# Lagged first layer with row scales from sums of squares, and a last block that finishes one token half early

## The chip, the core and the metric

The program runs on one core of a Trainium2 chip. The core's engines work from queues of their own: TensorE (PE in the profile, with its weight loads as PEld) multiplies, VectorE (DVE) and ScalarE (ACT) work on whole tiles, GpSimd (POOL) issues the indirect DMAs and some small steps, SyncE (SP) issues the other DMAs. The metric is device microseconds of one execution; lower is better. Times of stretches are microseconds from the start of the profiled span.

## The reference

Attention with landmarks over 8 batches and 8 heads gives 4608 rows of 512. A routed layer follows: each row goes to the one of 8 experts with the largest gate value. Then comes a dense layer with a squared ReLU.

```python
x = attention(q, k, v)                       # 4608 x 512
idx = argmax(x @ w_gate, axis=1); g = softmax(x @ w_gate)[idx]
for e in range(8):                           # first layer, D = 512, F = 1024
    out[idx == e] = g * (relu(x[idx == e] @ w1[e]) @ w2[e])
h = relu(out @ w_in)                         # second layer, F = 2048
y = (h * h) @ w_out
```

## The kernel before, in words

Every number of a matrix is kept as two float16 halves, high and low, so a product takes three matmuls: high by high, high by low, low by high.

The attention (`phase_a`) writes the rows to DRAM (`x_rows`) and works out a sorted order of rows by expert. It also runs two tiles of 128 rows of the first layer by itself ("the earlier tiles", names z, zvn, zkn).

`phase_m1` is the first layer: one step for each further tile of 128 rows, tile 2 to 37 with this data, 36 in all. The last two stand under run-time conditions. In a step, for tile j:

- GpSimd gathers the rows of tile j+3 (`gather`, L80).
- `prep` for tile j+2: a row scale from the largest magnitude (`rowscale`, L56 to L60, on DVE), the high half xh on ACT (L90), the low half on DVE (L92).
- SP turns the input of tile j+1 by a DMA transpose (`turn_dma`, L108). Tile 2 is turned on PE (`turn`, L101, L103).
- `mm1` (L120 to L122): 96 matmuls of 128 columns in two groups (hf 0 and 1). Behind each group ACT writes the high half of hT (L125, with the ReLU) and DVE the low half (L126).
- `mm2` (L135): 24 matmuls of 512 columns into py. For the first four hT tiles it runs high by high, low by high, high by low; for the other four, high by high, high by low, low by high.
- `post` for tile j-1: ACT takes py out with the gate (yg, L143), DVE finds a row scale from the largest magnitude (L56 to L60), ACT writes the high half (L149), DVE the factor (L153 to L156) and the low half (L157), GpSimd scatters the row tile into `x2` (L158).
- `change(j+1)`: where the next tile has another expert, ACT and DVE convert the staged weights (`conv`, L1045 and L1046, eight pieces each) into the one weight buffer wb, and SP loads the next expert's weights into the staging buffer. The condition is read at run time; with this data it holds at four tiles.
- `fill`: the second layer's weights come in as 64-bit numbers and are split beside the first layer, one load per step, in a generator in four parts (`wide_split`, L1065 to L1091): ACT clears the sign (fg), DVE builds the float32 bits, GpSimd makes sums of weight quarters (fq, L1087), ACT and DVE write the two halves.

Each engine works its queue strictly in the order in which the step emits; `go` and `run` advance the generators, so the order of those calls is the order of every queue.

`phase_m2` is the second layer: 18 blocks of 256 rows, 8 pairs of column groups per block, each with 24 matmuls (L1136 to L1138). `pair` squares the result and builds seven combinations hq; `piece`, two pairs later, multiplies them by seven weight combinations into seven sums (L1158); `result` adds the sums into two token halves and GpSimd scatters each half (`put`, L1174). The first block's input is loaded during the first layer (`first`, tile 16).

Of the kernel before, what the change touches and what calls it, by code (L numbers as in the profile page):

```python
# [52 lines left out]
def rowscale(nc, al, out, src, k, tag):  # L53
# [13 lines left out]
             pt=([128, 8, 128], F16), ph=([128, 4, 128], F32), py=([128, DM], F32))  # L67


class Layer1:  # L70
# [57 lines left out]
    def mm2(self, s):  # L128
        hT, (wh, wl) = s["hT"], self.w2
        s["py"] = py = self.al("py")  # L130

        hh, hl, lh = (0, wh), (0, wl), (1, wh)
        ps = [(f, *x) for f0, xs in ((0, (hh, lh, hl)), (4, (hh, hl, lh))) for x in xs for f in range(f0, f0 + 4)]
        for i, (f, a, w) in enumerate(ps):
            self.nc.tensor.matmul(py, hT[:, a, f], w[:, f], start=(i == 0), stop=(i == len(ps) - 1))  # L135
            if i % 4 == 3:
                yield

    def post(self, s, to, tok):
# [19 lines left out]
                                     in_=xr, in_offset=None)  # L159

# [775 lines left out]
def phase_m1(tc, cst, x_rows, x2, w1, w2, rt, stg, wb, fill, first):  # L936
    nc = tc.nc
    identh = cst["identh"]
    with (
        tc.tile_pool(name="m1", bufs=1, reuse_waits="tile") as m1,  # L940
        tc.tile_pool(name="m3", bufs=3, reuse_waits="tile") as m3,
        tc.tile_pool(name="m4", bufs=4, reuse_waits="tile") as m4,
        tc.tile_pool(name="m5", bufs=7, reuse_waits="tile") as m5,
        tc.tile_pool(name="mph", bufs=2, space=PSUM, reuse_waits="tile") as mph,
        tc.tile_pool(name="mpy", bufs=3, space=PSUM, reuse_waits="tile") as mpy,
# [17 lines left out]
        def change(j):  # L963
# [5 lines left out]
            for i in range(2):  # L969
                load(s["nx"], s["ld"], i)  # L970

        pools = dict(xg=m4, xm=m3, s1=m5, xh=m3, gt=m5, xT=m3, hT=m1, yg=m1, ym=m3, s2=m3, ss=m3, xr=m1,
                     ph=mph, py=mpy)
        L = Layer1(nc, cst, wb, x2, lambda nm: mph.tile(*TILES[nm], tag="ph", name=nm) if nm == "pt" else pools[nm].tile(*TILES[nm], tag=nm, name=nm))
# [13 lines left out]
        for j in range(PT, PT + 3):  # L988
            gather(j)
        for j in range(PT, PT + 2):  # L990
            run(L.prep(st[j]))
        run(L.turn(st[PT]))
        change(PT)
        idle = iter(())
        fls = [idle]
# [3 lines left out]

        def step(j):  # L1000
            last = j + 1 == NTL
            tail = j >= NTF
            po = L.post(st[j - 1], rt["sidx"][:, j - 1:j], rt["gidx"][:, j - 1:j]) if PT < j < NTF else idle
            pr = L.prep(st[j + 2]) if j + 2 < NTL else idle
            old, fl = fls.pop(), iter(() if tail else fill(j) or ())
            fls.append(fl)
            if not last:
                L.turn_dma(st[j + 1])
            if j == 4 + NE + PT + 2:
                first()  # L1010
            go(po, pr, po, fl)
            run(L.mm1(st[j], 0))
            if j + 3 < NTL:
                gather(j + 3)
            go(po)
            go(old, pr, po)
            run(L.mm1(st[j], 1))
            run(L.mm2(st[j]))
            if not last:
                change(j + 1)  # L1020
            go(fl, old, pr, fl)
            if j + 1 >= NTF:
                go(*(4 * [L.post(st[j], rt["sidx"][:, j:j + 1], rt["gidx"][:, j:j + 1])]))
# [32 lines left out]
def wide_split(tc, pool, w, scale, dst, quad=None):  # L1056
# [7 lines left out]
    g = pool.tile([128, 512], I32, tag="fg", name="fg")  # L1064
    nc.scalar.activation(g.bitcast(F32), hi.bitcast(F32), AF.Abs)  # L1065

    m = pool.tile([128, 512], I32, tag="fm", name="fm", bufs=1)
    V.tensor_scalar(m, lo, 29, 7, op0=ALU.logical_shift_right, op1=ALU.bitwise_and)
    yield
# [3 lines left out]
    yield  # L1073
# [29 lines left out]
def load_block(nc, pool, x2, blk):  # L1103

    n = TB // 128
    xT = pool.tile([128, 8, TB], F16, tag="x2T", name="x2T")
# [8 lines left out]
def phase_m2(tc, x2, wi, wo, first, out):  # L1115
# [4 lines left out]
    with (  # L1120
# [31 lines left out]
        def piece(b, f):  # L1152

            hq = ps[8 * b + f]["hq"]
            for k, (a, w) in enumerate(PRODS):
                for i, (u, x) in enumerate(((0, 0), (0, 1), (1, 0))):

                    PE.matmul(sums[k // 2][:, k % 2], hq[:, u, a], wo[:, x, f, w], start=(f == 0 and i == 0 and k % 2 == 0),  # L1158
                              stop=(f == 7 and i == 2), skip_group_check=True)

        def result(b):
# [4 lines left out]
            r = [n2.tile([128, TB], F32, tag=f"r{i}", name=f"r{i}") for i in range(3)]  # L1166
            p1, p6, p7, p5, p4, p3, p2 = (sums[k // 2][:, k % 2] for k in range(7))
# [4 lines left out]
            def put(t):  # L1172
                ACT.activation(o[t], o[t], AF.Copy, scale=sc[t])  # L1173
# [113 lines left out]
```

## Time and profile before

| | |
|---|---|
| time, three runs | 1443.92, 1450.49, 1451.67 us (median 1450.49) |
| profiled execution | 1445.92 us, span 1444.2 us |
| mean granted TensorE clock | 0.977 |
| busy share of the span | PE 94%, PEld 75%, DVE 72%, ACT 40%, POOL 19% |
| first layer, tile 2 to 37 | 290.5 to 716 us |
| second layer | 721 to 1433 us |

A timeline row gives the start, the duration, the engine, the line and the instruction with the tile it writes and the tiles it reads. The brackets give the idle time of that engine just before and what ended it. With several instructions merged (x8), the duration is from the first's start to the last's end. Successive instructions of an engine overlap a little, so their starts lie closer than their durations.

### The profile page before, as it was taken

How to read it: one execution, taken by the hardware profiler on the slowest of the kernel's cores; microseconds unless marked ns; L12 is line 12 of the kernel's file. 1: busy time of each engine (PE TensorE's matmuls, PEld its weight loads, DVE VectorE, ACT ScalarE, POOL GpSimd, SP SyncE). 2: the span in 40 equal slices, each digit the busy share in tenths (PEclk: the TensorE clock that was granted, in tenths of full speed). 3: DMA queues.
4: the chain of work that ended last, by engine and by line, in shares of the span. 5: the costliest groups of instructions: out<-in, count | busy, mean ns of one | idle time of the engine just before them, and what ended most of it. 6: DMA issues, size and time to landing. Idle time of an engine off the chain costs nothing. (4 is left out here: it accounts for less than half of the span.)

```text
span 1444.2 us, 35176 instructions
## 1 busy us (share of the span) xinstructions
PE 1352.3 (94%) x14312; PEld 1077.5 (75%) x14312; DVE 1040.5 (72%) x2651; ACT 575.8 (40%) x979; POOL 274.1 (19%) x282
## 2 busy tenths in 40 slices
PE   5999889889898997899899999999999999999996
PEld 4555555667575775667688888888888888888886
DVE  5888998858888887989556666666666666666664
ACT  4555565333553353443333333333333333333332
POOL 4434563111111223132200000000000000000000
PEclk9999999999999999999999999999999999999999
DMA  8767674476758547364310111111111101111100
GB/s 197 164 162 187 158 175 94 122 190 126 212 119 224 131 123 205 87 132 102 72 33 16 30 31 31 30 23 24 29 30 30 30 19 27 30 31 30 30 9 22
DMA packets 133695, 127.05 MB, mean 88 GB/s; under 512 B 90832, under 2 KB 109264, under 8 KB 133520
## 3 DMA queue, kind: packets, MB, share of 16 engines
q1 hardware_dynamic: 123680, 94.45, 28.5%
q0 software_dynamic: 9200, 30.21, 6.7%
q8 instruction: 114, 1.87, 0.6%
q14 instruction: 61, 0.50, 0.1%
q10 hardware_dynamic: 640, 0.02, 0.0%
HBM read 219.49 MB, written 28.89 MB: 172 GB/s over the span
## 5 line engine op out<-in xcount | busy, mean ns | idle before, releaser
L1158 PE MATMUL o<-wo,hq 128*128 128x256 f16 x3024 | 356.1, 272 | 0.0
L1158 PEld LDWEIGHTS <-hq 128*128 128x128 f16 x3024 | 295.6, 98 | 37.3 <-issue 2.8
L1136 PE MATMUL h<-x2T,wi 128*128 128x256 f16 x1152 | 314.8, 273 | 5.0 <-ACTq L1037 5.0
L1138 PE MATMUL h<-x2T,wi 128*128 128x256 f16 x1152 | 314.7, 273 | 0.0
L1137 PE MATMUL h<-x2T,wi 128*128 128x256 f16 x1152 | 314.7, 273 | 0.0
L1148 ACT ACTIVATE hq<-q 128x896 f16<-128x896 f32 x144 | 136.8, 950 | 289.9 <-DVE q L1146 289.9
L1150 DVE SCALAR_TENSOR_TENSOR hq<-q,hq 128x896 f16<-128x896 f32 x144 | 157.1, 1091 | 129.0 <-ACT hq L1148 129.0
L135 PE MATMUL py<-wb,hT 128*128 128x512 f16 x864 | 202.3, 392 | 22.2 <-DVE ss L153 16.3
L120 PE MATMUL ph<-xT,wb 128*128 128x128 f16 x1152 | 196.9, 220 | 8.7 <-DMA xT<-xh 6.8
L122 PE MATMUL ph<-xT,wb 128*128 128x128 f16 x1152 | 196.9, 220 | 3.4 <-DVE wb L1046 3.2
L121 PE MATMUL ph<-xT,wb 128*128 128x128 f16 x1152 | 196.9, 220 | 0.0
L1174 POOL DMA_INDIRECT out<-out,fa x36 | 54.5, 1514 | 665.3 <-ACT out L1173 590.6
L135 PEld LDWEIGHTS <-hT 128*128 128x128 f16 x864 | 84.9, 101 | 124.0 <-DVE hT L126 18.2
L1142 DVE TENSOR_TENSOR q<-q 128x512 f32<-128x512 f32 x144 | 99.5, 691 | 92.6 <-ACT q L1141 92.6
L1141 ACT ACTIVATE q<-h 128x512 f32<-128x512 f32 x144 | 85.4, 593 | 139.7 <-PE h L1138 139.7
L120 PEld LDWEIGHTS <-wb 128*128 128x128 f16 x1216 | 119.6, 98 | 14.8 <-issue 3.8
L1137 PEld LDWEIGHTS <-wi 128*128 128x128 f16 x1152 | 113.0, 98 | 16.2 <-issue 2.9
L1136 PEld LDWEIGHTS <-wi 128*128 128x128 f16 x1152 | 113.0, 98 | 15.7 <-SPq L1037 2.5
L1138 PEld LDWEIGHTS <-wi 128*128 128x128 f16 x1152 | 113.0, 98 | 13.4
L122 PEld LDWEIGHTS <-wb 128*128 128x128 f16 x1216 | 119.6, 98 | 4.4 <-DVE wb L1046 4.4
L121 PEld LDWEIGHTS <-wb 128*128 128x128 f16 x1216 | 119.6, 98 | 4.0
L126 DVE SCALAR_TENSOR_TENSOR hT<-ph,hT 128x512 f16<-128x512 f32 x72 | 49.7, 690 | 61.0 <-ACT hT L125 31.0
(289 smaller groups left out, 1904.8 us busy)
## 6 DMA issues: line engine op xcount, KB each, us to landing
stg<-in_moe_w SPq DMA_DIRECT2D x76, 2048.0 KB
qn<-in_q SPq DMA_DIRECT2D x16, 576.0 KB
kn<-in_k SPq DMA_DIRECT2D x16, 576.0 KB
vn<-in_v SPq DMA_DIRECT2D x16, 576.0 KB
fw<-in_moe_w_in SPq DMA_DIRECT2D x16, 512.0 KB
fw<-in_moe_w_out SPq DMA_DIRECT2D x16, 512.0 KB
x_rows<-xr SPq DMA_DIRECT2D x32, 192.0 KB
stg<-in_moe_w SPq DMA_DIRECT2D x16, 256.0 KB
```

Of the source, the lines that this page charges most:

```text
L120: nc.tensor.matmul(ph[:, f4], wh[:, c, fs], xT[:, c], start=(c == 0), stop=False)
L121: nc.tensor.matmul(ph[:, f4], wh[:, c, fs], xT[:, 4 + c], start=False, stop=False)
L122: nc.tensor.matmul(ph[:, f4], wl[:, c, fs], xT[:, c], start=False, stop=(c == 3))
L135: self.nc.tensor.matmul(py, hT[:, a, f], w[:, f], start=(i == 0), stop=(i == len(ps) - 1))
L1136: PE.matmul(ph[:, z], wi[:, 0, c, fs], xT[:, c], start=(c == 0), stop=False)
L1137: PE.matmul(ph[:, z], wi[:, 0, c, fs], xT[:, 4 + c], start=False, stop=False)
L1138: PE.matmul(ph[:, z], wi[:, 1, c, fs], xT[:, c], start=False, stop=(c == 3))
L1141: ACT.activation(q[:, 3:7], ph.rearrange("p z (t n) -> p (z t) n", t=2), AF.Relu, scale=2.0 ** -7)
L1142: V.tensor_tensor(q[:, 3:7], q[:, 3:7], q[:, 3:7], op=ALU.mult)
L1148: ACT.activation(hq[:, 0], q, AF.Copy, scale=0.5)
L1150: V.scalar_tensor_tensor(hq[:, 1], q, 0.5, hq[:, 0], op0=ALU.mult, op1=ALU.subtract)
L1158: PE.matmul(sums[k // 2][:, k % 2], hq[:, u, a], wo[:, x, f, w], start=(f == 0 and i == 0 and k % 2 == 0), stop=(f == 7 and i == 2), skip_ ...
```

## The change

`Stream1` replaces `Layer1` in `phase_m1`. The row scales come from sums of squares: ACT squares a row tile and adds up each row (`norm`), DVE makes two powers of two out of the sum by integer steps (`scales`), for one tile's input and another tile's output in one go. The output is no longer kept in yg: both halves are written from py with gate times scale. Gathers run four tiles ahead and scatters two behind, the turn by DMA two ahead, and PE turns tiles 2 and 3. `gate`, the factor and the token number move from DVE to GpSimd. Pools change with it: py 4, ph 3, fg 3.

```diff
-        ps = [... for f0, xs in ((0, (hh, lh, hl)), (4, (hh, hl, lh))) for x in xs for f in range(f0, f0 + 4)]
+        ps = [(f, *x) for x, f0 in ((hh, 0), (hl, 0), (hh, 4), (hl, 4), (lh, 0), (lh, 4)) for f in range(f0, f0 + 4)]
...
+    def norm(self, src, sq, i, scale=1.0):
+        self.nc.scalar.activation(self.al("jk"), src, AF.Square, scale=scale, accum_out=sq[:, i:i + 1])
+    def scales(self, sq, i, n, nm="s4"):
...
+        V.tensor_scalar(v, v, 1, 0x7F800000, op0=ALU.logical_shift_right, op1=ALU.bitwise_and)
+        V.tensor_scalar(o[:, i:i + n], v, -1.0, float(197 << 23), op0=ALU.mult, op1=ALU.add)
+        V.tensor_scalar(o[:, 2 + i:2 + i + n], v, 1.0, float(57 << 23), op0=ALU.mult, op1=ALU.add)
...
+    def yhigh(self, s):
+        s["xr"] = self.al("xr")
+        self.nc.scalar.activation(s["xr"][:, 0:DM], s["py"], AF.Copy, scale=s["gs"][:, 0:1])
+    def ylow(self, s):
+        xr = s["xr"]
+        self.nc.vector.scalar_tensor_tensor(xr[:, DM:2 * DM], s.pop("py"), s["gs"][:, 0:1], xr[:, 0:DM], ...)
...
         def step(j):
...
+            elif j + 4 < FAR:
+                gather(j + 4)
...
+            if j == NTF - 1:
                 first()
+            if PT + 2 <= j < NTF:
+                scatter(j - 2)
+            if j + 3 < FAR:
+                L.gate(st[j + 3])
+            up = [L.up(s, 0)]
+            go(up[0])
...
+                L.norm(st[j - 1]["py"], sq(j), 0, st[j - 1]["gt"][:, 0:1])
+                norm_x(j + 3)
+                L.low(st[j + 2])
+            go(fl)
...
+                s4 = L.scales(sums.pop(j), 0 if ny else 1, int(ny) + int(nx))
+                    L.out_scale(st[j - 1], nc.gpsimd)
...
+            up.append(L.up(s, 1))
+            go(up[1])
+            if j + 2 < NTF + 2:
+                L.turn_dma(st[j + 2])
+            run(L.mm2(s))
             if not last:
                 change(j + 1)
+            go(old, old)
+                L.yhigh(st[j - 1])
+                L.high(st[j + 3])
...
+            go(fl)
+                L.ylow(st[j - 1])
```

(The conditions `if ny`, `if nx` before some of these lines are left out here.) In `wide_split` the first `yield` moves ahead of DVE's first instruction, and a later one goes.

In the second layer, the last block is emitted in another order: `pair` 142 and 143 follow each other, the last three pieces first run the five products that the first finished token half needs, that half is added up and scattered, and then the other two products of the three pieces run. In `result` one more buffer keeps a partial sum, and for the last block the scale is put on the partial sums, so that one DVE instruction each finishes the other half. The inputs of the second layer's blocks now use the pool of the split's loads.

```diff
             if g >= LAG:
+                if g == NP - 2:
+                    next(rest, None)
+                    continue
+                if g == NP - 1:
+                    piece(NB - 1, 4)
+                b, f = divmod(g - LAG, 8)
+                end = b == NB - 1 and f >= 5
+                piece(b, f, range(5) if end else range(7))
+                if f == 7:
+                    res = result(b)
+                    next(res)
+                    for f in range(5, 8) if end else ():
+                        piece(b, f, (5, 6))
+                    next(res, None)
...
+            last = b == NB - 1
...
+            if last:
+                V.scalar_tensor_tensor(o[0][:, 1], p3, sc[0], r[3], op0=ALU.mult, op1=ALU.add)
+                V.scalar_tensor_tensor(o[0][:, 0], p2, sc[0], r[0], op0=ALU.mult, op1=ALU.add)
```

What the change moves is seen in the queues. On ACT, from one weight conversion (wb<-stg) to the second high half of hT; before:

```order
L1045 ACTIVATE wb<-stg 128x1024 x8
L966 UNCONDITIONAL_BRANCH x2
L143 ACTIVATE yg<-py,gt 128x512
L1065 ACTIVATE fg<-fw 128x512
L125 ACTIVATE hT<-ph 128x512
L149 ACTIVATE xr<-yg,s_6368 128x512
L1089 ACTIVATE wi<-fg 128x512
L90 ACTIVATE xh<-xg,s_6362 128x512
L125 ACTIVATE hT<-ph 128x512
```

And now:

```order
L1179 ACTIVATE wb<-stg 128x1024 x8
L1030 UNCONDITIONAL_BRANCH x2
L1222 ACTIVATE wi<-fg 128x512
L207 ACTIVATE xr<-py,gs 128x512
L187 ACTIVATE xh<-xg,s_6213 128x512
L127 ACTIVATE hT<-ph 128x512
L169 ACTIVATE jk,sq<-py,gt 128x512
L169 ACTIVATE jk,sq<-xg 128x512
L1199 ACTIVATE fg<-fw 128x512
L127 ACTIVATE hT<-ph 128x512
```

The split's fg step and yg stood ahead of the first high half; now the two halves of the output and the input (xr, xh) and the end of a split (wi) do, and two squares (jk) stand between the high halves.

On DVE, the last twelve rows up to the first low half of hT behind a conversion; five more stand between the conversion and these. Before:

```order
L94 COPY gt<-xg 128x1
L1081 SCALAR_TENSOR_TENSOR fg<-fw,fg 128x512
L56 TENSOR_REDUCE xm<-xg 128x1
L57 TENSOR_SCALAR xm<-xm 128x1
L59 TENSOR_SCALAR xm<-xm 128x1
L60 TENSOR_SCALAR s_6362<-xm 128x1
L56 TENSOR_REDUCE ym<-yg 128x1
L57 TENSOR_SCALAR ym<-ym 128x1
L59 TENSOR_SCALAR ym<-ym 128x1
L60 TENSOR_SCALAR s_6368<-ym 128x1
L1068 TENSOR_SCALAR fm<-fw 128x512
L126 SCALAR_TENSOR_TENSOR hT<-ph,hT 128x512
```

And now, from the conversion on:

```order
L1180 SCALAR_TENSOR_TENSOR wb<-stg,wb 128x1024 x8
L1030 UNCONDITIONAL_BRANCH x2
L1224 SCALAR_TENSOR_TENSOR wi<-fg,wi 128x512
L1203 TENSOR_SCALAR fm<-fw 128x512
L1204 TENSOR_SCALAR fg<-fg 128x512
L1205 TENSOR_SCALAR fg<-fg 128x512
L1206 SCALAR_TENSOR_TENSOR fg<-fg,fm 128x512
L1214 SCALAR_TENSOR_TENSOR fg<-fw,fg 128x512
L211 SCALAR_TENSOR_TENSOR xr<-py,gs,xr 128x512
L128 SCALAR_TENSOR_TENSOR hT<-ph,hT 128x512
```

The two reductions with their small steps went, and the first low half is now the eighth instruction behind the conversion.

On ACT ahead of the first layer (z and zvn are the last earlier tile's, xh and xT tiles 2 and 3); before:

```order
L90 ACTIVATE xh<-xg,s_4692 128x512
L143 ACTIVATE z_3837<-py,zvn 128x512
L90 ACTIVATE xh<-xg,s_4703 128x512
L149 ACTIVATE zvn<-z_3837,zvn 128x512
L103 ACTIVATE xT<-pt 128x1024
```

And now:

```order
L145 ACTIVATE z_3837<-py,zvn 128x512
L1043 TENSOR_LOAD s_79 x3
L1044 TENSOR_LOAD s_79
L169 ACTIVATE jk,sq<-xg 128x512
L187 ACTIVATE xh<-xg,s_4709 128x512
L151 ACTIVATE zvn<-z_3837,zvn 128x512
L169 ACTIVATE jk,sq<-xg 128x512
L187 ACTIVATE xh<-xg,s_4718 128x512
L105 ACTIVATE xT<-pt 128x1024 x2
```

The earlier tile's evacuation (z) came between the two tiles' high halves; now it and four register loads stand ahead of both, with two squares, and both tiles are turned on PE.

## Rows read from the trace of the kernel before

**Rows 1.** Timeline of ACT, line L143; start, duration (us), then engine and instruction

```profile
303.11 0.69 ACT L143 ACTIVATE yg<-py,gt 128x512 f32<-128x512 f32 x1 [4.58 <-PE py L135]
...
316.76 0.69 ACT L143 ACTIVATE yg<-py,gt 128x512 f32<-128x512 f32 x1 [4.58 <-PE py L135]
...
358.92 0.69 ACT L143 ACTIVATE yg<-py,gt 128x512 f32<-128x512 f32 x1 [4.58 <-PE py L135]
...
388.66 0.69 ACT L143 ACTIVATE yg<-py,gt 128x512 f32<-128x512 f32 x1 [5.45 <-PE py L135]
...
461.78 0.69 ACT L143 ACTIVATE yg<-py,gt 128x512 f32<-128x512 f32 x1 [4.58 <-PE py L135]
...
525.02 0.69 ACT L143 ACTIVATE yg<-py,gt 128x512 f32<-128x512 f32 x1 [3.97 <-PE py L135]
...
590.24 0.69 ACT L143 ACTIVATE yg<-py,gt 128x512 f32<-128x512 f32 x1 [4.46 <-PE py L135]
...
621.36 0.69 ACT L143 ACTIVATE yg<-py,gt 128x512 f32<-128x512 f32 x1 [5.40 <-PE py L135]
...
716.27 0.69 ACT L143 ACTIVATE yg<-py,gt 128x512 f32<-128x512 f32 x1 [3.30 <-PE py L135]
```

**Rows 2.** Timeline of PE, first layer: tile 3 and the first weight change

```profile
306.03 0.22 PE L120 MATMUL ph<-xT,wb 128*128 128x128 f16 x1 [2.96 <-DMA xT<-xh]
...
370.55 0.23 PE L122 MATMUL ph<-xT,wb 128*128 128x128 f16 x1 [0.51 <-DVE wb L1046]
...
378.44 1.04 PE L135 MATMUL py<-wb,hT 128*128 128x512 f16 x4 [2.98 <-ACT hT L125]
...
381.79 6.84 PE L135 MATMUL py<-wb,hT 128*128 128x512 f16 x20 [2.31 <-DVE ss L153]
```

**Rows 3.** Window with the first weight change: us, busy us by engine, clock, DMA

```profile
374.00:386.00 12.00, 6.72 (x41) 3.06 (x39) 11.12 (x28) 3.48 (x6) 1.96 (x2) 0.74 1.06 352
```

**Rows 4.** Timeline of ACT at the first weight change

```profile
364.78 7.67 ACT L1045 ACTIVATE wb<-stg 128x1024 f16<-128x1024 f32 x8
...
377.24 0.66 ACT L1065 ACTIVATE fg<-fw 128x512 f32<-128x512 f32 x1 [4.22 <-issue]
```

**Rows 5.** Timeline of DVE at the first and the third weight change

```profile
365.86 9.17 DVE L1046 SCALAR_TENSOR_TENSOR wb<-stg,wb 128x1024 f16<-128x1024 f32 x8 [0.25 <-ACT wb L1045]
...
381.05 0.68 DVE L126 SCALAR_TENSOR_TENSOR hT<-ph,hT 128x512 f16<-128x512 f32 x1
...
532.08 10.14 DVE L1046 SCALAR_TENSOR_TENSOR wb<-stg,wb 128x1024 f16<-128x1024 f32 x8 [0.17 <-issue]
```

**Rows 6.** Timeline of PE: its first matmul of each layer

```profile
290.52 0.29 PE L120 MATMUL ph<-xT,wb 128*128 128x128 f16 x1 [1.90 <-ACTq L966]
...
721.13 0.37 PE L1136 MATMUL h<-x2T,wi 128*128 128x256 f16 x1 [4.96 <-ACTq L1037]
```

**Rows 7.** Timeline of PE: the end of the program

```profile
1425.92 7.18 PE L1158 MATMUL o<-wo,hq 128*128 128x256 f16 x63
```

**Rows 8.** Groups of DVE: count, busy us and mean ns of one, idle before

```profile
L1091 DVE SCALAR_TENSOR_TENSOR wo<-fq,wo 128x1792 f16<-128x1792 f32 x8 | 16.2, 2020 | 0.1
...
L60 DVE TENSOR_SCALAR s<-ym 128x1 int32<-128x1 int32 x36 | 5.5, 153 | 1.2
```

**Rows 9.** Groups of ACT: the exponential with a row sum

```profile
L401 ACT ACTIVATE eC<-pc,mx 128x288 f32<-128x288 f32 x32 | 15.7, 496 | 5.8 <-DVE mx L399 4.0 <-DVE rb L335 1.8
...
L401 ACT ACTIVATION_READ_ACCUMULATOR eC<-pc,mx 128x1 f32 x32 | 6.4, 199 | 0.0
```

**Rows 10.** Timeline of ACT before the first layer

```profile
285.58 0.67 ACT L143 ACTIVATE z<-py,zvn 128x512 f32<-128x512 f32 x1
```

**Rows 11.** Timeline of GpSimd at the third weight change

```profile
532.60 1.72 POOL L1087 TENSOR_TENSOR fq<-fq 128x256 f32<-128x256 f32 x1
```

**Rows 12.** Timeline of GpSimd: the last two scatters

```profile
1436.37 0.98 POOL L1174 DMA_INDIRECT out<-out,fa  x1 [26.71 <-issue]
...
1439.88 0.97 POOL L1174 DMA_INDIRECT out<-out,fa  x1 [2.53 <-DMA out<-out,fa]
```

More of the change, by code (lines that the diff above doesn't have):

```diff
@@ L987, in phase_m1, with sq, norm_x @@
             regs(j)
-        for j in range(PT, PT + 3):
+        sums = {}
+        def sq(j):
+            if j not in sums:
+                sums[j] = L.al("sq")
+            return sums[j]
+        def norm_x(j):
+            L.norm(st[j]["xg"][:, 0:DM], sq(j - 3), 1)
+        for j in range(PT, PT + 4):
             gather(j)
         for j in range(PT, PT + 2):
-            run(L.prep(st[j]))
-        run(L.turn(st[PT]))
-        change(PT)
-        idle = iter(())
-        fls = [idle]
+            norm_x(j)
+            st[j]["sx"] = L.scales(sums.pop(j - 3), 1, 1)
+            L.high(st[j])
+        for j in range(PT, PT + 2):
+            L.gate(st[j])
+            L.low(st[j])
+            run(L.turn(st[j]))
+        change(PT)
+        norm_x(PT + 2)
+        st[PT + 2]["sx"] = L.scales(sums.pop(PT - 1), 1, 1)
+        L.gate(st[PT + 2])
+        L.high(st[PT + 2])
+        fls = [iter(())]
         def go(*gens):
@@ L1002, in step @@
             tail = j >= NTF
[L1003 to L1004 removed]
             old, fl = fls.pop(), iter(() if tail else fill(j) or ())
             fls.append(fl)
[L1007 removed]
+            s = st[j]
+            near = FAR <= j + 2 < NTL
+            if near:
+                gather(j + 2)
+            elif j + 4 < FAR:
+                gather(j + 4)
@@ new lines, in step @@
+            if near:
+                t = L.al("sqy")
+                n = st[j + 2]
+                L.norm(n["xg"][:, 0:DM], t, 1)
+                n["sx"] = L.scales(t, 1, 1)
+                L.gate(n)
+                L.high(n)
+                L.low(n)
+            go(fl)
+            if ny:
+                L.ylow(st[j - 1])
+            if j + 1 >= NTF:
+                if not tail:
+                    scatter(j - 1)
+                t = L.al("sqy")
+                L.norm(s["py"], t, 0, s["gt"][:, 0:1])
+                s["sy"] = L.scales(t, 0, 1, "s4y")
+                L.out_scale(s, nc.vector)
+                L.yhigh(s)
+                L.ylow(s)
+                scatter(j)
@@ L1100, with load_block @@
 PRODS = ((5, 5), (1, 1), (6, 6), (0, 0), (4, 2), (2, 4), (3, 3))
-def load_block(nc, pool, x2, blk):
+def load_block(nc, wide, pool, x2, blk):
     n = TB // 128
-    xT = pool.tile([128, 8, TB], F16, tag="x2T", name="x2T")
+    xT = wide.tile([128, 512, 2], I32, tag="fw", name="x2T").rearrange("p a b -> p (a b)").bitcast(F16).rearrange("p (c t) -> p c t", c=8)
     for t in range(n):
@@ L1112, in load_block, with phase_m2 @@
     return xT, fa
-def phase_m2(tc, x2, wi, wo, first, out):
+def phase_m2(tc, x2, wi, wo, wide, first, out):
     nc = tc.nc
@@ L1150, in pair, with total, piece @@
             V.scalar_tensor_tensor(hq[:, 1], q, 0.5, hq[:, 0], op0=ALU.mult, op1=ALU.subtract)
-        def piece(b, f):
+        def total(k):
+            k += k > 4
+            return sums[k // 2][:, k % 2]
+        def piece(b, f, ks=range(7)):
             hq = ps[8 * b + f]["hq"]
-            for k, (a, w) in enumerate(PRODS):
+            for k in ks:
+                a, w = PRODS[k]
                 for i, (u, x) in enumerate(((0, 0), (0, 1), (1, 0))):
-                    PE.matmul(sums[k // 2][:, k % 2], hq[:, u, a], wo[:, x, f, w], start=(f == 0 and i == 0 and k % 2 == 0),
+                    PE.matmul(total(k), hq[:, u, a], wo[:, x, f, w], start=(f == 0 and i == 0 and k in (0, 2, 4, 5)),
                               stop=(f == 7 and i == 2), skip_group_check=True)
@@ L1165, in result @@
             o = [n2.tile([128, 2, TB], F32, tag=f"out{t}", name=f"out{t}") for t in range(2)]
-            r = [n2.tile([128, TB], F32, tag=f"r{i}", name=f"r{i}") for i in range(3)]
-            p1, p6, p7, p5, p4, p3, p2 = (sums[k // 2][:, k % 2] for k in range(7))
+            r = [n2.tile([128, TB], F32, tag=f"r{i}", name=f"r{i}") for i in range(4)]
+            p1, p6, p7, p5, p4, p3, p2 = map(total, range(7))
             def add(to, x, y):
@@ L1234, in moe_kernel @@
             tc.tile_pool(name="x0", bufs=1, reuse_waits="tile") as x0,
+            tc.tile_pool(name="wide", bufs=2, reuse_waits="tile") as wide,
             tc.manual_schedule(),
```

105 lines of the change are left out of this document (72 added, 33 removed).

## The prediction

> **What bounds the kernel now.** The busy shares in the table above name TensorE (PE) first; the question is where it stops. I read ACT's L143 rows, because each starts when PE has finished a tile of the first layer [rows 1]. From 461.78 to 525.02 lie six tiles: 10.54 us each, which is PE's own time for 96 + 24 matmuls, since no PE wait falls there. Against that pitch 303.11 to 316.76 (one tile) is 3.11 too long, 358.92 to 388.66 (two) 8.66, 388.66 to 461.78 (six) 9.88, 525.02 to 590.24 (five) 12.52 and 590.24 to 621.36 (two) 10.04; 621.36 to 716.27 (nine) has nothing. That is 44.2 us in 35 tiles, 41.1 of it at the four places where an expert's weights are converted (32 conversions of 8 each) and the tile behind them.
>
> PE's own waits in that layer say what ends them [rows 2]: 2.96 for tile 3's turned input, and at the first weight change 0.51 for the converted weights, 2.98 for the high half of hT, and 2.31 for its low half (the name in that row, DVE ss, is the instruction right behind the low half in DVE's queue). The window row there shows a granted clock of 0.74 [rows 3]: PE worked 6.72 of 12 us, and part of that at 1.2 instead of 2.4 GHz, which is in the 8.66. The queues explain the order: ACT converts from 364.78 for 7.67, then its split step (fg) comes only at 377.24, and hT's high half stands behind it [rows 4]; DVE converts from 365.86 for 9.17 and reaches the low half at 381.05, six us of other work later [rows 5]. The second layer runs on PE from 721.13 to 1433.1 with no wait that counts [rows 6, 7], so only its start and its end can give.
>
> **The change, part by part.** All against the profiled execution, 1445.92 us (span 1444.2).
>
> *A tile without a weight change: 0.* PE's 120 matmuls stay. DVE loses two reductions, nine small steps and two copies per tile and gains three small ones of 0.15 [rows 8]. ACT loses yg and gains two squares with a row sum. The trace has no square; the nearest is the exponential with a row sum, 0.50 for 288 columns and 0.20 for the read of the sum [rows 9]. Below, it is a plain pass over 512 columns, 0.67 [rows 10], plus 0.20; above, 0.50 x 512/288 + 0.20 = 1.08. I take 0.85 (passes overlap by some 0.08). A matmul of 512 columns counts as four of 128, so the pitch gives 10.54 / 192 = 0.055 and 0.22. From the start of a tile hT's first high half starts at 2.75 (behind PE's first 48 matmuls); then come two squares and the split's first step, so the second high half starts at 2.75 + 0.5 + 1.7 + 0.55 = 5.5 and ends at 6.1. In the new order of the second product PE wants it behind eight matmuls, at 96 x 0.055 + 8 x 0.22 = 7.03. So 0.9 of cover hides the squares; by the upper bound 0.6 is left. If the cover goes, each further us per tile costs 34.
>
> *A weight change: from 41.1 to 11.2.* The conversions stay, 0.1 later. First change, in the trace's times. ACT is free at 372.5, and has three steps (0.52, 0.62, 0.61) ahead of the first high half, which ends at 374.85; the squares and the split step put the end of the second at 377.55. The split step no longer waits for DVE, since its buffers are three now. DVE is free at 375.1; ahead of the first low half it has seven steps, 3.7 us, so that half ends at 379.5, and the second, behind xh's low half and three small steps, at 381.35. PE ends the first product at 375.5 (0.6 of waiting for weights is in that), runs the high half's eight matmuls to 377.2, waits 0.4, runs eight more to 379.35, waits 0.25, four to 380.5, waits 0.95, and ends at 382.4. Two tiles at the pitch from 358.92 would end at 380.0: 2.4 lost, with rounding 2.5, where 8.66 was. The same for the second change. At the third no earlier split is left to finish, and the low half stands 0.6 sooner: 1.6, and 1.0 more if the conversion takes 10.14 again [rows 5]: 2.6. At the fourth the finish is the large one, 2.02 on DVE [rows 8] instead of 0.68, and about 1.1 more on ACT: 3.65. Sum 11.2; 29.9 gained. What is late next is the second low half of hT, on DVE. The tiles behind a change (1.2 and 3.0 in the trace, for the turned input) lose nothing, since the turn is issued a tile sooner: low half of xh at 380, up to 4.9 us under the weight load, needed after 390.
>
> At that third place the rows show the conversion 0.97 longer where a GpSimd subtraction of 1.72 lies beside it [rows 5, 11]. The Trainium skill (SBUF — State Buffer, "SBUF: two separate sides") says that a DVE step with two SBUF inputs and a GpSimd step exclude each other for a whole instruction; the trace agrees in direction. In the changed order the four subtractions come behind the conversion: by the rule it would take 9.17, and xh's low half would wait for one subtraction, 0.8; the third change would then cost 2.4 and not 2.6.
>
> *The start: 0.4 lost.* Tile 3 is now turned by PE before the weights, so its 3.11 goes. But both tiles' inputs are prepared behind ACT's evacuation of the last earlier tile (285.58, 0.67 [rows 10]), four register loads, and a square, three small steps, a high half, another scale, a square, three small steps, a low half, four turns and a copy: 286.25 + 0.85 + 0.6 + 0.7 + 0.7 + 0.85 + 0.6 + 0.7 + 0.5 + 1.0 = 292.75, and the loads. These no row shows; 0 to 1.9 (PE's idle time before its first matmul [rows 6]), I take 1.1. PE starts at about 293.9 and not at 290.52: 3.4 to 3.5 late.
>
> *Into the second layer: 0.5 lost.* PE there waits for the last tile's tail, 4.96 [rows 6]. It waited for ACT; now it waits for DVE, one pass later in the chain (0.75), while the sum on ACT replaces a longer reduction on DVE. Between 0.3 gained and 1 lost.
>
> *The end: 1.1 gained.* 63 matmuls take 7.18 [rows 7], 0.11 each. For the last block the products of the first token half end 18 matmuls before PE does instead of 6, so its first scatter can start 12 x 0.11 = 1.3 sooner. The second scatter stays 3.5 behind the first [rows 12], since it waited for that one's landing, and what prepares it is hidden by that. PE's last piece waits some 0.2 for hq, as two pairs now run back to back. From 0 to 2.5.
>
> *At nothing:* the small GpSimd steps and the earlier gathers (GpSimd idles most of a tile), the first block's input loaded at tile 35 instead of 16 (20 us before its use), the earlier tiles' product order. If GpSimd's steps became late, ACT's yhigh would wait, then the next high half; the lag gives them half a tile.
>
> Sum: 29.9 - 0.4 - 0.5 + 1.1 = 30.1, so 1415.8 for an execution like the profiled one. That one stands 4.6 below the median of the three timed runs (1450.49) and 2.1 below the mean of all four (1448.0); I add 2.1: **1418**.
>
> **Rivals.** *Weight changes keep half their price* (chance 0.18). DVE still has seven steps between the conversion and the first low half, and PE still idles there; if the four stops stay long enough for the clock to fall, each costs 5 to 6 instead of 2.8: 10 to 13 more, about 1430. For it: the clock row [rows 3]. Against: the three stops of 0.25 to 0.95 have matmuls between them.
>
> *ACT becomes the bound* (0.06), slower than before. Two squares per tile, one of them from PSUM to PSUM: if each takes more than 0.85 + 0.45, PE waits for the second high half in every tile. The gain of 30 is used up at 0.9 us per tile (34 tiles), so at 1.75 a square; at 2.2 it is 1.8 a tile, 61 us, so 1479. Against it: the exponential's rows [rows 9] are far below.
>
> *It shifts the stops and saves nothing that can be told* (0.03): the turned inputs or gathers come late from GpSimd or behind the weight loads. Against: each is issued at least a tile sooner. About 1448.
>
> *The changes cost almost nothing* (0.08): conversions overlap better, and the two layers' start is no later: 1405 to 1408.
>
> **How the numbers follow.** The forecast has 0.65: 1418, its own range 1411 to 1424 (the start 1, the second layer's start 0.8, the end 1.3, the changes 3, and the runs differ by up to 4). The wide range reaches down to 1408 and up to 1433, which takes in most of the first rival. Faster by over 0.5% (about what can be told from no change here): 0.91; within it: 0.03; slower: 0.06.
>
> **What would show it.** L143 is gone; the evacuations of the tiles on ACT (L207) should keep 10.54 and the four pairs around a conversion be 1.5 to 4 too long. PE's longest waits in the first layer should be under 1.6, for hT's halves, with no wait for a turned input, and the granted clock should stay at 1.0 behind a change. The first matmul of tile 2 should come at 293 to 295. A pitch over 10.6, or squares over 1.4 us, would make the forecast wrong; so would PE stops of 3 us at the conversions.

## The result and the profile after

The changed kernel takes 1427.05 us (median of 5 runs, 1421.22 to 1429.41) where the kernel before takes 1448.63 (5 runs): a ratio of 0.9858, 95% interval 0.9834 to 0.9883. It is 21.6 faster; 30 was forecast, and 1418. The time lies outside the forecast's own range (1411 to 1424) and inside its wide one (1408 to 1433). Its profiled execution is its fastest, 1421.22 with a span of 1419.5.

Part of the difference between the two profiled executions is not the change's. PE's second product of the last earlier tile but one, ahead of which nothing is changed, starts at 266.99 before and at 263.70 after. In the 14 profiled executions of this study it starts between 263.70 and 272.21. So 3.3 of the 24.7 between the two spans came before the change acts; 21.4 is left, close to the 21.6 of the medians. By stage, from that start on (the common point below):

| stage | before | after | gained | forecast |
|---|---|---|---|---|
| to PE's start of tile 3 | 39.04 | 39.79 | -0.75 | -0.4 |
| four weight changes and the tiles behind them, over 10.54 a tile | 41.1 | 16.4 | 24.7 | 29.9 |
| PE's wait into the second layer | 4.96 | 5.38 | -0.4 | -0.5 |
| second layer, PE's first to last matmul | 711.7 | 713.9 | -2.2 | 0 |
| PE's last matmul to the end | 11.1 | 10.9 | 0.2 | 1.1 |

PE of the changed kernel at the start (start, duration, instruction, in brackets idle time before it and what ended it):

```profile
288.27 2.10 PE L103 MATMUL pt<-identh,xh 128*128 128x128 f16 x16 [6.39 <-DVE s L178]
291.59 0.29 PE L122 MATMUL ph<-xT,wb 128*128 128x128 f16 x1 [1.22 <-ACTq L1030]
303.49 0.22 PE L122 MATMUL ph<-xT,wb 128*128 128x128 f16 x1
```

Both tiles are turned in one go, tile 2 starts 4.4 later after the common point (3.4 was forecast), and tile 3 follows in 11.90 instead of 15.51 [rows 2, 6]. PE idles 6.39 ahead of the turns, and the granted clock (third column from the right) is at its lower level, 0.50 or 1.2 GHz, for longer than before. The kernel before, then the changed one:

```profile
287.70:294.30 6.60, 4.70 (x44) 4.43 (x44) 3.73 (x17) 2.24 (x3) 1.34 (x2) 0.50 1.03 375
```

```profile
284.30:294.40 10.10, 4.86 (x43) 4.36 (x44) 3.81 (x17) 6.05 (x10) 2.68 (x5) 0.50 1.06 360
```

The lower level reaches 2.9 into tile 2 here (3.9 before), and 2.7 to 5.6 in the variants of the changed kernel below. In those, the way from the common point to tile 3 is 0.6 to 2.2 longer than the 39.04 of before (3.0 with the squares doubled), so the 0.75 in the table is near the low end.

PE's first matmul of a tile, around the first change (tiles 9, 10, 11, 12) and the third (23 to 26):

```profile
366.73 0.22 PE L122 MATMUL ph<-xT,wb 128*128 128x128 f16 x1
379.55 0.22 PE L122 MATMUL ph<-xT,wb 128*128 128x128 f16 x1
391.45 0.22 PE L122 MATMUL ph<-xT,wb 128*128 128x128 f16 x1
401.99 0.22 PE L122 MATMUL ph<-xT,wb 128*128 128x128 f16 x1
...
520.20 0.22 PE L122 MATMUL ph<-xT,wb 128*128 128x128 f16 x1
533.23 0.22 PE L122 MATMUL ph<-xT,wb 128*128 128x128 f16 x1
548.20 0.22 PE L122 MATMUL ph<-xT,wb 128*128 128x128 f16 x1
558.74 0.22 PE L122 MATMUL ph<-xT,wb 128*128 128x128 f16 x1
```

401.99 - 391.45 is the pitch, 10.54, as before. The tile with the change is 2.28 too long, and the one behind it 1.36; at the third change 2.49 and then 4.43. The second and fourth cost 2.27 and 3.61, with nothing behind. PE's stops in these four tiles:

```profile
368.01 0.23 PE L124 MATMUL ph<-xT,wb 128*128 128x128 f16 x1 [0.50 <-DVE wb L1180]
377.00 1.04 PE L137 MATMUL py<-wb,hT 128*128 128x512 f16 x4 [0.47 <-DVE hT L128]
378.67 1.04 PE L137 MATMUL py<-wb,hT 128*128 128x512 f16 x4 [0.63 <-DVEq L1030]
387.99 1.25 PE L137 MATMUL py<-wb,hT 128*128 128x512 f16 x5 [1.19 <-ACTq L1030]
...
532.35 1.04 PE L137 MATMUL py<-wb,hT 128*128 128x512 f16 x4 [1.45 <-DVEq L1030]
543.05 5.31 PE L137 MATMUL py<-wb,hT 128*128 128x512 f16 x16 [2.58 <-ACTq L1030]
```

In the tile with the change, behind 0.50 for the weights, only stops of 0.47 and 0.63 (1.45 at the third change) for DVE's low halves are left, where 2.98 and 2.31 stood [rows 2]. In the tile behind it PE stops again, for ACT. The granted clock stays at 1.00 (2.4 GHz) around the first change, where it was 0.74 [rows 3], and falls behind the third:

```profile
366.00:379.00 13.00, 11.40 (x123) 7.56 (x121) 12.70 (x20) 9.28 (x17) 3.70 (x5) 1.00 0.68 250
...
533.00:548.00 15.00, 12.42 (x122) 8.07 (x121) 11.56 (x19) 5.58 (x12) 7.17 (x14) 0.89 0.91 221
```

ACT in tile 10 and in tile 24, what stands ahead of the second high half:

```profile
386.79 0.66 ACT L1199 ACTIVATE fg<-fw 128x512 f32<-128x512 f32 x1 [2.34 <-DMA fw<-in_moe_w_in]
387.35 0.58 ACT L127 ACTIVATE hT<-ph 128x512 f16<-128x512 f32 x1
...
541.24 0.60 ACT L169 ACTIVATE jk<-xg 128x512 f32<-128x512 f32 x1 [2.30 <-DMA xg<-x_rows,gidx]
541.87 0.64 ACT L1199 ACTIVATE fg<-fw 128x512 f32<-128x512 f32 x1
542.42 0.58 ACT L127 ACTIVATE hT<-ph 128x512 f16<-128x512 f32 x1
```

Both wait for a transfer: a piece of the second layer's weights in tile 10, the gathered rows of tile 27 in tile 24. SP issued the piece at 375.72, behind the next expert's weights, 4 MB from 368.46 on. GpSimd shows why the gather is late:

```profile
528.69 2.65 POOL L1220 TENSOR_TENSOR fq<-fq 128x256 f32<-128x256 f32 x3 [12.54 <-DVE fq L1214]
531.50 1.01 POOL L82 DMA_INDIRECT xg<-x_rows,gidx  x1 [0.16 <-issue]
```

Three of the split's four subtractions wait for DVE, which converts first, and the gather stands behind them. It landed at 541.16, 9.7 after its issue; the two gathers before it took 3.4 and 4.5. DVE there, the conversion and two later steps beside the subtractions:

```profile
516.79 9.17 DVE L1180 SCALAR_TENSOR_TENSOR wb<-stg,wb 128x1024 f16<-128x1024 f32 x8 [0.25 <-ACT wb L1179]
...
529.73 1.04 DVE L191 SCALAR_TENSOR_TENSOR xh<-xg,s,xh 128x512 f16<-128x512 f32 x1
530.69 0.68 DVE L176 TENSOR_SCALAR sq<-sq 128x2 int32<-128x2 int32 x1
```

### The profile page after: what moved, and what is told of

Its sections match the earlier page's. It is cut to its first block, busy times and chain, and to the rows that moved or that the text cites. A ratio compares the mean times of both kernels' runs of the same rounds, so it can differ in the third digit from the quotient of the medians.

```text
span 1419.5 us, 35252 instructions
## 1 busy us (share of the span) xinstructions
PE 1342.6 (95%) x14320; PEld 1073.0 (76%) x14320; DVE 960.0 (68%) x2299; ACT 607.4 (43%) x1093; POOL 336.3 (24%) x460
## 4 chain that ended last, share of the span: by engine, by line
PE 43%; DVE 4%; issue 2%; ACT 2%; DMA 0%; POOLq 0%; DVEq 0%; ACTq 0%
PE o L1296 20%; PE h L1269 8%; PE h L1271 8%; PE h L1270 8%; DVE r L1308 1%; DVE q L1275 1%; ACT q L1274 1%; DVE out L1308 1%; ACT r L1315 0%; DVE q L1279 0%; DVE q L1276 0%; DVE q L1277 0%; DVE q L1278 0%; ACT hq L1281 0%; DMA out<-out,fa 0%
## 5 line engine op out<-in xcount | busy, mean ns | idle before, releaser
L137 PE MATMUL py<-wb,hT 128*128 128x512 f16 x864 | 196.3, 382 | 9.7 <-ACTq L1030 4.4
```

## The experiments

The brackets behind a time give its ratio to the kernel before, timed beside it, and the 95% interval of that ratio. "Excess" is the sum over 10.54 a tile at the four changes and behind them, in the profiled execution: 41.1 before, 16.4 after. A tile "behind" a change is the next one.

**Two additions exchanged.**

```diff
-            add(r[3], p5, r[1])
             add(r[2], p7, r[1])
+            add(r[3], p5, r[1])
```

> The changed kernel with two additions in result exchanged (r[2] ahead of r[3]). In the changed kernel PE takes 714.20 us from its first to its last matmul of the second layer, in the kernel before 711.97; every block's first piece is 0.13 later. Theory A: the step that frees the second bank (out = p5 + r[2]) now stands right behind the step that makes r[2], and a step that needs the one just ahead of it starts about 0.1 late; with one step between them again PE's stretch is 712.0 to 712.3, so 2 us less of 1427. Rival B: the added seventh addition per block by itself is what makes the bank late; then the stretch stays at 714.2.

Measured: 1427.51 (0.9848, 0.9804 to 0.9893). The median doesn't tell, since executions of one kernel differ by more than the 2 us in question; the trace does. PE's first and last matmul start of the second layer, per line: the changed kernel,

```profile
L1269 PE MATMUL h<-x2T,wi x1152: 272/273/418, 694.4 to 1398.5; 128*128 128x256 f16 x192
L1296 PE MATMUL o<-wo,hq x3024: 269/273/283, 703.6 to 1408.3; 128*128 128x256 f16 x189
```

and with the additions exchanged:

```profile
L1269 PE MATMUL h<-x2T,wi x1152: 272/273/417, 703.1 to 1404.9; 128*128 128x256 f16 x192
L1296 PE MATMUL o<-wo,hq x3024: 269/273/282, 712.2 to 1414.7; 128*128 128x256 f16 x189
```

713.9 and 711.6 (before: 711.7). DVE's additions at one block's end in the changed kernel,

```profile
742.05 1.28 DVE L1308 TENSOR_TENSOR r<-o,r 128x256 f32<-128x256 f32 x3 [1.29 <-ACT r L1315]
743.37 1.42 DVE L1308 TENSOR_TENSOR out<-o,r 128x256 f32<-128x256 f32 x4
```

and exchanged:

```profile
750.67 1.28 DVE L1308 TENSOR_TENSOR r<-o,r 128x256 f32<-128x256 f32 x3 [1.29 <-ACT r L1315]
751.87 1.41 DVE L1308 TENSOR_TENSOR out<-o,r 128x256 f32<-128x256 f32 x4
```

The fourth addition frees the bank that PE wants next. It starts 1.32 behind the first where it needs the result just ahead of it, and 1.20 where another step lies between. The 0.12 shows in PE, at each of 17 block ends. Theory A holds.

**Two buffers for fg.**

```diff
-    g = pool.tile([128, 512], I32, tag="fg", name="fg", bufs=3)
+    g = pool.tile([128, 512], I32, tag="fg", name="fg")
```

> The changed kernel with two instead of three buffers for the split's fg. Theory A: at each weight change ACT's split step waits again for DVE's last step on an old buffer, behind the conversion, and the second high half of hT stands behind it: the four pairs cost 3 more each, PE's waits there name ACT's hT, and the time is 9 to 13 above the changed kernel, 1436 to 1440; tiles without a change keep 10.54. Rival B: the low halves on DVE are late by more than that anyway, and the buffers give nothing: 1425 to 1429.

Measured: 1428.76 (0.9858, 0.9814 to 0.9902); the changes 2.28, 2.26, 2.49, 3.60, as with three. Theory A falls. At the first change ACT's split step starts at 376.90 right behind the squares, and the DVE step that it would have waited for had ended at 376.56:

```profile
376.90 0.67 ACT L1199 ACTIVATE fg<-fw 128x512 f32<-128x512 f32 x1
```

```profile
375.88 0.68 DVE L1224 SCALAR_TENSOR_TENSOR wi<-fg,wi 128x512 f16<-128x512 f32 x1
```

That step is now the first behind the conversion; before, three others stood ahead of it.

**The old order of the second product.**

```diff
-        ps = [(f, *x) for x, f0 in ((hh, 0), (hl, 0), (hh, 4), (hl, 4), (lh, 0), (lh, 4)) for f in range(f0, f0 + 4)]
+        ps = [(f, *x) for f0, xs in ((0, (hh, lh, hl)), (4, (hh, hl, lh))) for x in xs for f in range(f0, f0 + 4)]
```

> The changed kernel with the second product in the order of before (hh, lh, hl for the first half; hh, hl, lh for the second). Theory A: PE wants the first low half behind four matmuls and not behind sixteen, so at each weight change it waits some 2.8 instead of 0.5 for it; four changes cost 1.7 each more with the clock kept, up to 4 where it falls: 1434 to 1443. Rival B: the order only moves the wait from one matmul to another, the last low half ends the tile at the same time: within 2 of 1427. Tiles without a change stay at 10.54 by both.

Measured: 1436.55 (0.991, 0.9883 to 0.9938). The changes cost 5.69, 5.51, 3.46 and 7.79, and 0.65 behind the third: excess 23.1. PE at the first change:

```profile
380.06 3.17 PE L137 MATMUL py<-wb,hT 128*128 128x512 f16 x7 [3.20 <-DVE hT L128]
```

One stop of 3.20 in place of 0.47 and 0.63. Theory A, though the tiles behind lose less (0 at the first two changes).

**The gather ahead of the split.**

```diff
-            elif j + 4 < FAR:
+            elif j == PT:
                 gather(j + 4)
...
+            if j + 5 < FAR:
+                gather(j + 5)
             go(fl)
```

> The changed kernel with each tile's gather issued ahead of the split's steps of the tile before, not behind them. Theory A: at the third change the gather of tile 27 was issued only at 531.5, behind four subtractions of GpSimd that wait for DVE's conversion, and landed at 541.2 under the weight load; ACT's square waited 2.30 for it and PE 2.58, the clock fell to 0.89, and the tile behind the change was 4.43 too long. With the gather ahead it is issued near 520 and lands before the load: that tile costs 0 to 1, 3.5 to 4.4 less in all. Rival B: it lands late under the weight load wherever it is issued, or ACT's wait for the output scale (3.42 there) takes its place: the tile keeps 3 or more. The other three changes stay as they are (2.3 + 1.4, 2.3, 3.6).

Measured: 1424.82 (0.9835, 0.9786 to 0.9884). The third change costs 3.16 and nothing behind it, where it was 2.49 and 4.43; excess 13.5. Theory A in this execution; the run of both edits below shows that a second transfer can take its place, and the medians (1424.82 and 1427.05) lie closer than the runs of one kernel. The third change itself costs 0.7 more: GpSimd now reaches the first subtraction beside DVE's conversion (523.23, 1.71 instead of 0.72), and the conversion takes 9.90 instead of 9.17.

**The split's first step behind the half.**

```diff
-            go(fl)
...
             go(up[1])
+            go(fl)
```

> The changed kernel with the split's first step on ACT behind the second high half of hT, not ahead of it. Theory A: in the tile behind the first change (and in some executions the second) that step waits for its piece of the second layer's weights, which lies in the DMA queue behind the 4 MB of the next expert, and hT's second high half stands behind it; with the half first those tiles lose nothing (now 1.36 and 0 in the profiled execution, 0.6 to 1.6 in others), the tile behind the third change keeps its 4, the pairs at the changes stay at 2.3, 2.3, 2.5 and 3.6 or fall by 0.3: 1 to 3 us less than 1427. Rival B: the half is late for another reason (its square, or DVE's low half), and these tiles keep what they lose.

Measured: 1426.19 (0.9852, 0.9818 to 0.9887); excess 21.0 in the profiled execution, which took 1433.76, while the other four took 1425.62 to 1426.64. Theory A falls there: the tiles with a change rise to 2.84, 2.83, 3.07 and 4.75 (PE's wait for the weights is 0.80, not 0.50), and behind the first change, where 1.29 is still lost, PE waits for its turned input instead:

```profile
399.71 0.22 PE L122 MATMUL ph<-xT,wb 128*128 128x128 f16 x1 [1.13 <-DMA xT<-xh]
```

**Squares twice.**

```diff
-        self.nc.scalar.activation(self.al("jk"), src, AF.Square, scale=scale, accum_out=sq[:, i:i + 1])
+        for _ in range(2):
+            self.nc.scalar.activation(self.al("jk"), src, AF.Square, scale=scale, accum_out=sq[:, i:i + 1])
```

> The changed kernel with each of the two squares per tile on ACT done twice. Theory A: in a tile without a change the second high half ends at 6.16 us from the tile's start and PE wants it at 7.03; the two squares measure 0.80 + 0.63 from start to start, so 1.43 more make it 0.5 late: a pitch of 11.0 to 11.1 where 10.54 was, in some 30 tiles, 14 to 18 us more, 1441 to 1446. Rival B (the prediction's size, 0.85 a square): 1.7 more, 0.8 late, 25 us, 1452. Rival C: ACT's slack is larger than the cover says and the pitch stays 10.54: 1427 to 1430.

Measured: 1450.13 (1.0008, 0.9985 to 1.0031), the whole gain of the change. In each of the tiles 3 to 34 PE stops at the ninth matmul of the second product:

```profile
329.05 3.63 PE L137 MATMUL py<-wb,hT 128*128 128x512 f16 x16 [0.31 <-ACTq L1031]
```

and the pitch without a change is 11.02 to 11.04. That is theory A's half microsecond; the total is 4 above its range, since the changes cost more too (2.8, 2.8, 2.9, 4.0 over this pitch, and 1.4, 1.1 and 5.8 behind the first three).

**The kernel before, split step behind both halves.**

```diff
-            go(po, pr, po, fl)
+            go(po, pr, po)
...
             run(L.mm1(st[j], 1))
+            go(fl)
```

> The kernel before with the split's first step (ACT's fg and DVE's fm) issued behind both halves of hT and not ahead of them. At the first change PE waited 2.98 for hT's high half, which stood behind that step on ACT, and then 2.31 for the low half on DVE. Theory A: the two waits lie one behind the other only on paper; DVE's low half comes at 381.05 minus 0.42 whatever ACT does, so each change gains 0.4 to 1, the PE wait for the low half grows to 4 to 5 and the whole gains 1 to 4 of 1448. Rival B: the wait for the high half is the price, and without it each change gains 3: 1436 to 1438.

Measured: 1450.71 (1.0026, 0.9999 to 1.0053), excess 41.5. PE at the first change:

```profile
383.19 7.02 PE L135 MATMUL py<-wb,hT 128*128 128x512 f16 x20 [5.13 <-DVE hT L126]
```

The wait for the high half (2.98) is gone and the one for the low half is 5.13 instead of 2.31. The mechanism is theory A's; its gain of 1 to 4 did not come.

**The last block as before.** The second layer's function is that of the kernel before, but for where the first block's input comes from.

```diff
-                if g == NP - 2:
...
-                piece(b, f, range(5) if end else range(7))
-                if f == 7:
-                    res = result(b)
...
+                piece(*divmod(g - LAG, 8))
+                if (g - LAG) % 8 == 7:
+                    result((g - LAG) // 8)
```

> The changed kernel with the second layer's sums, order and last block as in the kernel before (the first layer stays changed). Theory A: PE's stretch in the second layer goes back from 714.2 to 711.8 to 712.0, the first scatter starts 3.3 behind PE's end and not 0.6, and the second 3.5 behind it: the end ties (6.8 and 6.7 behind PE's end), so the whole is 2 us less than the changed kernel: the edit of the last block lost 2 us and did not gain 1. Rival B: the 3.1 us of issue that the second scatter waits in the changed kernel, and not before, belongs to its place in GpSimd's longer program; then it stays with the old block, and the end is 3 later: 1 us more than the changed kernel.

Measured: 1427.58 (0.9871, 0.9834 to 0.9908). PE's stretch is 712.0. The last two scatters and PE's last piece, here,

```profile
1414.77 0.96 POOL L1307 DMA_INDIRECT out<-out,fa  x1 [25.85 <-ACT out L1306]
1420.86 0.97 POOL L1307 DMA_INDIRECT out<-out,fa  x1 [5.12 <-issue]
```

```profile
1405.80 7.17 PE L1291 MATMUL o<-wo,hq 128*128 128x256 f16 x63
```

and in the changed kernel:

```profile
1409.19 0.96 POOL L1311 DMA_INDIRECT out<-out,fa  x1 [24.96 <-ACT out L1324]
1415.28 0.97 POOL L1311 DMA_INDIRECT out<-out,fa  x1 [5.13 <-issue]
```

```profile
1405.02 3.56 PE L1296 MATMUL o<-wo,hq 128*128 128x256 f16 x31 [0.25 <-DVE hq L1283]
```

The new block starts the first scatter 0.6 behind PE's end, the old one 1.8: 1.2 gained. (The kernel before had 3.3 [rows 7, 12]; the other 1.5 came with either block, and no run shows why.) But both have 6.1 between the scatters, the kernel before 3.5 [rows 12]. Rival B on that point: the gap doesn't come from the last block's edit.

**Additions and gather together** (the two diffs above).

> The changed kernel with the two additions exchanged and each gather ahead of the split's steps of the tile before. Theory A (both causes as the single runs showed them, and they add): PE's stretch in the second layer 712.0 instead of 714.2, the tile behind the third change 0 to 0.1 too long instead of 4 with the pair 0.7 longer, so 5.5 to 6 less than the changed kernel: 1420 to 1422. Rival B: the time is set elsewhere and the median moves by less than 3.

Measured: 1422.94 (0.9828, 0.9801 to 0.9854). Less came than the sum, 4.1 by the medians for 5.5 to 6, so between A and B. PE's stretch is 712.0, as A has it. But the excess is 16.1, hardly below 16.4: the tiles behind the first two changes lost 1.34 and 1.51, and the one behind the third 1.94, for a piece of weights that came late:

```profile
546.89 0.66 ACT L1201 ACTIVATE fg<-fw 128x512 f32<-128x512 f32 x1 [2.24 <-DMA fw<-in_moe_w_out]
```

**And the halves first on DVE.**

```diff
-            if j + 2 < FAR:
-                L.low(st[j + 2])
             go(fl)
-            if ny or nx:
...
             up.append(L.up(s, 1))
             go(up[1])
+            if j + 2 < FAR:
+                L.low(st[j + 2])
+            if ny or nx:
...
```

> As the run with exchanged additions and earlier gathers, and the low half of xh and the three small scale steps on DVE come behind hT's second low half, not ahead of it. Theory A: of what a change still costs (2.3, 2.3, 3.2, 3.6) PE's last wait of 0.63 for the second low half goes, 0.5 to 1 each: 2 to 4 less, 1417 to 1419. Rival B: what comes later instead (GpSimd's output scale, the turned input of the tile after next, ACT's yhigh) holds the next tile, and nothing is gained or some is lost: 1420 to 1424.

Measured: 1428.62 (0.9855, 0.983 to 0.9881), 5.7 slower than without by the medians. The changes cost 2.33, 2.33, 2.65 and 3.66: the last wait of 0.63 went, and the weights came 0.40 + 0.79 late instead of 0.50. So theory A falls. The tiles behind the first three lost 7.32, 1.90 and 2.37, and in each ACT waited for a piece of weights (5.15, 2.81 and 1.47), which is none of the causes that rival B names; no run shows whether the edit made these later or the execution did.

**And each piece asked for one tile sooner.**

```diff
-            tc.tile_pool(name="wide", bufs=2, reuse_waits="tile") as wide,
+            tc.tile_pool(name="wide", bufs=3, reuse_waits="tile") as wide,
...
-                            pend[j + 1] = (wide_load(tc, wide, src, 512), sc, dst, qd)
+                            pend[i + PT + 1] = (wide_load(tc, wide, src, 512), sc, dst, qd)
...
+                        for i in (0, 1) if j == PT else (j - PT + 1,):
+                            ask(i)
```

> As the run with exchanged additions and earlier gathers, and each piece of the second layer's weights is asked for one tile sooner (three buffers for the pieces, two for fg, which cost nothing, and fewer of the small ones). Theory A: the piece that the tile behind the first and the second change waited for is then ahead of the next expert's 4 MB in the DMA queue, ACT's step does not wait, and these tiles lose nothing where they lost 1.2 and 1.0: 2 less, 1418 to 1420. Rival B: the turned input, which goes through the same queue behind the 4 MB, takes its place with 1.1 to 1.3, as where the step was moved behind the half: 1420 to 1422.

Measured: 1420.93 (5 runs, 1418.61 to 1422.01; 0.9799, 0.9776 to 0.9822). The changes cost 2.27, 2.27, 3.16 and 3.60, and behind them 0, 0, 0.20 and 0: excess 11.5. Theory A: the piece for tile 10 is now issued at 359.80, ahead of the 4 MB (372.26), ACT's step in that tile waits for nothing, and PE has no wait for its turned input:

```profile
388.15 0.66 ACT L1201 ACTIVATE fg<-fw 128x512 f32<-128x512 f32 x1
```

This version beats both kernels.

**The kernel before with the new order of the second product.** The diff of the old order, reversed.

> The kernel before with the changed kernel's order of the second product, and nothing else. Theory A: at a change PE then wants the low halves last, but the second high half (382.64 on ACT at the first change, behind a step that waits for DVE) comes late as well: PE runs eight matmuls at 378.4, waits some 3 for that half, and ends 1 to 2 sooner than before: 4 to 8 in all, 1440 to 1444. Rival B: the order alone gives back what it costs to undo it in the changed kernel, 9: 1438 to 1440. Rival C: the late halves set the end whatever the order: 1447 to 1449.

Measured: 1446.04 (0.9989, 0.9963 to 1.0015); excess 38.8. At the first change PE stops for the first high half and then for the second:

```profile
378.24 2.89 PE L135 MATMUL py<-wb,hT 128*128 128x512 f16 x8 [2.97 <-ACT hT L125]
383.07 4.97 PE L135 MATMUL py<-wb,hT 128*128 128x512 f16 x16 [1.94 <-ACTq L966]
```

Between A and C: 2.3 of excess gained, not 4 to 8. The order needs the high halves early, and the old queues still bring the second one late.

## Why the prediction was right, and where it was not

*Right.* A tile without a change stayed at 10.54. The squares measure 0.80 and 0.63 from start to start, 1.43 where 1.7 was taken, and the second high half ends at 6.16 (6.1 forecast); doubling them showed the edge of the cover where the sum had it. The tiles with a change cost 2.28, 2.27, 2.49 and 3.61 against 2.5, 2.5, 2.6 and 3.65, and the wait behind the conversion is DVE's low halves, as said. The ways into both layers were within 0.4 of the forecast in the profiled execution, though the sum has no term for the lower clock in tile 2, which made the first one up to 1.4 longer in other executions. The last block's first scatter starts 1.2 sooner than with the old block (1.3).

*The step that failed: "The tiles behind a change ... lose nothing", and with it "At nothing: the small GpSimd steps and the earlier gathers".* I looked for the wait that the trace of before had in those tiles, the turned input, and saw it go. I did not ask which other transfers ACT's queue now waits for ahead of hT's second half. Two do: the square of a gathered row, and the split's step on a piece of weights. Both lie behind work that the change sets off, GpSimd's subtractions and the next expert's 4 MB, and cost 5.8 in the profiled execution; in three others with the same queues in the first layer (additions exchanged, two buffers, last block as before) the tile behind the first change alone lost 0.6 to 5.25. In every variant of the changed kernel but the one with the split's step behind the half, each tile that lost more than 0.2 behind one of the first three changes had ACT waiting for one of these transfers. With both transfers issued earlier the excess is 11.5, and the sum had 11.2. Three of the prediction's own signs tell of the same step: PE's longest wait in the first layer was 2.58 and not under 1.6, the clock fell to 0.89 behind the third change, and that change with the tile behind it cost 6.9 and not 1.5 to 4.

*The second term: the second layer "with no wait that counts".* I took the edit of `result` for one of the last block. It also reorders the additions of every block, and 0.13 at each of 17 makes 2.2. Exchanging two lines takes it back.

*The third: "The second scatter stays 3.5 behind the first".* It is 6.1. The old block shows the same, so it is not the edit that I priced. The chain of waits of the changed kernel (start, duration) shows the first scatter's transfer and then 3.09 (0.52 in the kernel before) in which GpSimd waits for nothing that the profile records:

```profile
1409.19 2.73 DMA out<-out,fa
...
1411.97 3.09 issue
```

No packet is on any DMA queue in that time. What it is stays open; I made no run that shortens GpSimd's program.

*A wrong reason with a right number: the split step "no longer waits for DVE, since its buffers are three now".* Two do as well; the finishing step's place behind the conversion does it. And PE's wait behind that step, 2.98, the largest at the first change, was worth nothing by itself: taken away alone, the low half filled it. What gained the 24.7 is several parts at once. The product's order alone gains 2.3 of excess, everything without the order 18.0 (41.1 - 23.1), and both 24.7. No run splits the 18.0 further.

*The price of the Trainium skill's rule* (SBUF — State Buffer, "SBUF: two separate sides"): the third conversion took 9.17, as the rule had it, with no GpSimd subtraction beside it. Behind it, beside the subtractions, xh's low half took 1.04 instead of 0.74 and the first scale step 0.68 instead of 0.17, 0.8 together, as long as the one wait that I gave that half. The change cost 2.49, between 2.4 by the rule and 2.6 without it. Where the gather was moved, one subtraction did lie beside the conversion, and the conversion took 9.90: the trace agrees again.

*The rivals.* The time, 1427, lies nearer to the rival in which the changes keep half their price (1430) than to the forecast, and they kept 0.40 of it. That rival's place was wrong all the same: not PE's short stops in the tile with the change (10.6 in all, where the forecast had 11.2), but the next tile.

## What to carry to other kernels

When the waits around a long step on two engines are cut, list every transfer and every queue that starts late because of it, one tile further on, and issue those ahead of it. A wait in the trace is worth what is late right behind it, so take it away alone before it is given a price. Where a step is moved within a helper that runs in every block, price every block.

## What the runs showed of the hardware

- A DVE addition of 128x256 that needs the result just ahead of it starts 0.12 later than one with a step between them.
- Three one-column steps of GpSimd, which take 0.20, 0.27 and 0.18 in many tiles of the changed kernel, took 0.99, 2.18 and 1.19 beside DVE's conversion at the first change (and the same at the second and the fourth):

```profile
363.61 0.99 POOL L217 TENSOR_TENSOR iv<-s,s 128x1 f32<-128x1 f32 x1
364.69 2.18 POOL L218 TENSOR_SCALAR xr<-iv 128x1 f32<-128x1 f32 x1
366.82 1.19 POOL L219 COPY xr<-gidx 128x1 int32<-128x1 int32 x1
```

- In the 14 profiled executions PE reached the second product of the last earlier tile but one up to 8.5 us apart (263.70 to 272.21), with the same code ahead of it. Two profiled executions are compared from there on.
